# Values of all but the last tile in a loop on TensorE with register addresses, in one column group

## The chip, the cores and the metric

The kernel runs on one core of a Trainium2 chip. The metric is the device time of that core in microseconds (us). Three runs of the kernel before gave 1252.83 us in the median, from 1252.80 to 1253.23 us.

## The reference

Attention with a single query row per head: 8 batches times 32 heads are 256 independent heads, each with one query of 128 numbers and 4096 keys and values, all in bf16.

```python
scale = q.shape[-1] ** -0.5
scores = jnp.einsum('bhqd,bhkd->bhqk', q, k) * scale
attn = _softmax(scores, axis=-1)
return jnp.einsum('bhqk,bhkd->bhqd', attn, v)
```

Keys and values are 268 MB each, and every byte of them is used once. The result has 256 rows of 128 numbers.

## The kernel before

**Tiles.** The work goes in 32 tiles (`NT`) of 8 heads (`G`). In a tile each of the 128 partitions holds 256 keys (`C`) of one head, so that 16 partitions make up a head, and a tile of K or of V is 128 partitions by 32768 bf16 numbers, 8.4 MB. K tiles live in two buffers and V tiles in one (`KB, VB = 2, 1`); only the last V tile is put into a K buffer.

**Scores, in quarters of 64 keys.** For each quarter VectorE multiplies K by the query, in place (L179), and folds the 128 products of a key to 64 (L182), in the first two quarters to 32 (L187). TensorE adds up what is left by matmuls with the identity as weights into a PSUM tile `ps` (`sum_over_d`, L199): four matmuls of 512 columns for each of the first two quarters and eight for each of the last two. VectorE reduces `ps` to scores (`scores_of`, L211). The last three tiles fold to 64 throughout.

**Weights.** When a tile has all its scores, VectorE finds the maximum and the bias (L221 to L232), and ScalarE takes eight exponentials (L240), one per head, into `w`. A partition's weights are zero for the heads that it doesn't belong to.

**Values.** `values_of` (L250 to L268) makes 64 matmuls for a tile. Each takes four keys of every partition: the weights are the 32 columns of `w` for 4 keys times 8 heads, the moving operand is 512 columns of V, and the output is 32 partitions by 512 columns of the PSUM tile `av`. Consecutive matmuls go to four different groups of 32 partitions of `av` (`c0 // CB % TG`), which are four column groups of the array. ScalarE copies `av` to `comb` (L292), and four small matmuls with the selection matrix `pick` (L307) take out the useful quarter-blocks and add the four groups. For every second tile `norm_of` and `recip_of` make the normaliser, and `finish_of` scales the result and stores it now and then.

**Order.** `tc.manual_schedule()` keeps the order of the code on every engine. In the loop over t (L328 to L362) TensorE has, for a tile t: the sums of quarter 0, the query of tile t+1, the sums of quarter 1, the 64 value matmuls of tile t-1, the sums of quarters 2 and 3, and the small matmuls of tile t-1. In tiles 30 and 31 (`v_last`) the values of t-1 come after all four sums. VectorE goes from quarter to quarter, with the reduction of a quarter one quarter behind. SyncE (SP) issues all loads, in the order K(t+1), V(t), K(t+2), V(t+1). V(t) waits until the last value matmul of t-1 has read the single V buffer, K(t+2) until the sums of tile t are through.

Of the kernel before, what the change touches and what calls it, by code (L numbers as in the profile page):

```python
# [7 lines left out]
ACT = mybir.ActivationFunctionType  # L8
# [3 lines left out]
F32 = mybir.dt.float32  # L12

G = 8
KB, VB = 2, 1
TG = 4
R = 2
OB = 4
LAST = 4
NEG = -1.0e30  # L20


@with_exitstack
def kernel(
# [7 lines left out]
    nc = tc.nc  # L32
    B, H, Sq, D = q.shape
    S = k.shape[2]
    P = nc.NUM_PARTITIONS
# [3 lines left out]
    C = S // PH  # L39
    NT = NH // G  # L40
# [5 lines left out]
    CB = 4  # L46
    RG = R * G
    NQ = NT // R
    TB = 32
    AG = CB * G  # L50
    assert TG * AG == P and NH % P == 0 and P % G == 0 and TB % PH == 0 and C % CB == 0

    q_n = q.rearrange("b h o d -> (b h o) d").rearrange("(x p) d -> p x d", p=P)
# [13 lines left out]
    ps_v = ctx.enter_context(tc.tile_pool(name="ps_v", bufs=2, space=bass.MemoryType.PSUM))  # L67
# [9 lines left out]
        out=ident[:], in_=ident[:], pattern=[[-1, P]], compare_op=ALU.not_equal,  # L77
# [32 lines left out]
    for j in range(TG):  # L110
# [17 lines left out]
    nc.gpsimd.memset(w_last[:], 0.0)  # L128

    loads = {}  # L130
    cuts = {
        ("k", 0): [C // 2] * 2,
        ("k", NT - 3): [C // 2] * 2,
# [5 lines left out]
    def load(kind, t):  # L139
        src = k_t if kind == "k" else v_t  # L140
        home = "v" if kind == "v" and t < NT - 1 else "k"
        pool = k_pool if home == "k" else v_pool
        buf = pool.tile([P, C, D], BF16, name=f"{kind}t", tag=home)
        c0 = 0
        for n in cuts.get((kind, t), [C]):
            nc.sync.dma_start(buf[:, c0 : c0 + n, :], src[t, :, c0 : c0 + n, :])  # L146
            c0 += n
            if kind == "k" and t == 0 and c0 == n:
                nc.sync.dma_start(q_all[:], q_n)
        assert c0 == C  # L150
        loads[kind, t] = buf
# [3 lines left out]
    def q_prep(t):  # L155
        x, p0 = divmod(t * G, P)
        qh = ps_q.tile([G, D], F32, name="qh", tag="qp")
        nc.tensor.matmul(  # L158
            qh[:], lhsT=ident[:, p0 : p0 + G], rhs=q_all[:, x, :], start=True, stop=True
        )  # L160
        qg = q_pool.tile([G, D], BF16, name="qg", tag="qg")
        nc.scalar.activation(out=qg[:], in_=qh[:], func=ACT.Copy)  # L162
        qp = ps_q.tile([P, D], F32, name="qp", tag="qp")
        nc.tensor.matmul(qp[:], lhsT=heads[:].rearrange("g h x -> g (h x)"), rhs=qg[:], start=True, stop=True)  # L164
        qb = q_pool.tile([P, 1, D], BF16, name="qb", tag="qb")
        nc.scalar.activation(out=qb[:, 0, :], in_=qp[:], func=ACT.Copy)  # L166
        qbs[t] = qb
# [6 lines left out]
    def product(t, lo, hi):  # L174
        kt = loads["k", t]
        qb = qbs[t]
        for c0 in range(lo, hi, MC):
            part = kt[:, c0 : c0 + MC, :]
            nc.vector.tensor_tensor(  # L179
                out=part, in0=part, in1=qb[:].to_broadcast([P, MC, D]), op=ALU.mult  # L180
            )
            nc.vector.tensor_tensor(  # L182
                out=part[:, :, 0 : D // 2], in0=part[:, :, 0 : D // 2],
                in1=part[:, :, D // 2 : D], op=ALU.add,
            )
            if width_of(t, c0 // UC) < D // 2:
                nc.vector.tensor_tensor(  # L187
                    out=part[:, :, 0 : D // 4], in0=part[:, :, 0 : D // 4],
                    in1=part[:, :, D // 4 : D // 2], op=ALU.add,
                )  # L190
# [3 lines left out]
    def sum_over_d(t, u):  # L194
        kt = loads["k", t]
        ps = ps_s.tile([P, UC, DS], F32, name="ps", tag="ps")
        n = width_of(t, u) // DS
        for s in range(n):
            nc.tensor.matmul(  # L199
                ps[:], lhsT=ident[:],  # L200
                rhs=kt[:, u * UC : (u + 1) * UC, s * DS : (s + 1) * DS],
                start=(s == 0), stop=(s == n - 1),
            )
        sums[t, u] = ps
# [3 lines left out]
    def scores_of(t, u):  # L208
        if u == 0:
            scs[t] = sc_pool.tile([P, C], F32, name="sc", tag="sc")  # L210
        nc.vector.tensor_reduce(  # L211
            out=scs[t][:, u * UC : (u + 1) * UC], in_=sums.pop((t, u))[:], axis=AX.X, op=ALU.add
        )

    ws = {}
# [30 lines left out]
            nc.gpsimd.tensor_copy(out=w_last[:, :, RG - G : RG], in_=w[:, C - LAST : C, :])  # L246

    avs = {}

    def values_of(t, lo, hi):  # L250
        vt = loads["v", t]
        w = ws[t]
        if lo == 0:
            avs[t] = ps_v.tile([P, CB * D], F32, name="av", tag="av")
        end = C if t < NT - 1 else C - LAST


        group = [
            0 if t == NT - 1 and C // 2 <= c0 < C // 2 + 3 * C // 16 else c0 // CB % TG
            for c0 in range(0, end, CB)  # L260
        ]
        for c0 in range(lo, hi, CB):
            i = c0 // CB
            j = group[i]
            nc.tensor.matmul(  # L265
                avs[t][j * AG : (j + 1) * AG, :], lhsT=w[:, c0 : c0 + CB, :],
                rhs=vt[:, c0 : c0 + CB, :], start=(i < TG), stop=(j not in group[i + 1 :]),
            )  # L268
# [6 lines left out]
    def norm_of(n):  # L275
        zp = ps_z.tile([RG, 1], F32, name="zp", tag="zp")
        nc.tensor.matmul(  # L277
            zp[:], lhsT=esums.pop(n).rearrange("p r g -> p (r g)"), rhs=ones[:],
            start=True, stop=True,
        )  # L280
        zps[n] = zp

    def recip_of(n):
        rzs[n] = small.tile([RG, 1], F32, name="rz", tag="rz")
        nc.vector.reciprocal(out=rzs[n][:], in_=zps.pop(n)[:])  # L285
# [3 lines left out]
    def copy_of(t):  # L289
        comb = small.tile([P, CB, D], BF16, name="comb", tag="comb")  # L290
        av = avs.pop(t)[:].rearrange("p (m d) -> p m d", d=D)
        nc.scalar.activation(out=comb[:], in_=av, func=ACT.Copy)  # L292
        combs[t] = comb

    def result_of(t):
        n, r = divmod(t, R)
        comb = combs.pop(t)
        if r == 0:
            ops[n] = ps_o.tile([RG, D], F32, name="op", tag="op")
        if t == NT - 1:  # L300
            for i in range(LAST):
                nc.tensor.matmul(
                    ops[n][:], lhsT=w_last[:, i, :], rhs=loads["v", t][:, C - LAST + i, :],
                    start=False, stop=False,
                )
        for m in range(CB):
            nc.tensor.matmul(  # L307
                ops[n][:], lhsT=pick[:, m, r, :], rhs=comb[:, m, :],
                start=(r == 0 and m == 0), stop=(r == R - 1 and m == CB - 1),
            )  # L310

    def finish_of(n):
        s, u = divmod(n, OB)
        if u == 0:
            stages[s] = o_pool.tile([RG, OB, D], BF16, name="stage", tag="stage")
        nc.scalar.activation(  # L316
            out=stages[s][:, u, :], in_=ops.pop(n)[:], func=ACT.Copy, scale=rzs.pop(n)[:, 0:1]
        )
        last = s == NQ // OB - 1
        if u == OB - 1 or (last and u == OB - 2):  # L320
            lo = u if (last and u == OB - 1) else 0
            nc.scalar.dma_start(o_n[s, :, lo : u + 1, :], stages[s][:, lo : u + 1, :])

    Q = C // 4
    load("k", 0)
    with tc.manual_schedule():
        q_prep(0)
        for t in range(NT):  # L328
            v_last = t >= NT - 2
            n = t // R - 1  # L330
            if t + 1 < NT:
                load("k", t + 1)
            load("v", t)
            product(t, 0, Q)
            sum_over_d(t, 0)
            if t > 2 and t % R == 1:
                recip_of(n)
                finish_of(n)
            if t + 1 < NT:
                q_prep(t + 1)  # L340
            product(t, Q, 2 * Q)
            sum_over_d(t, 1)
            scores_of(t, 0)
            if t > 0 and not v_last:
                values_of(t - 1, 0, C)
                copy_of(t - 1)
            product(t, 2 * Q, 3 * Q)
            sum_over_d(t, 2)
            scores_of(t, 1)
            product(t, 3 * Q, C)  # L350
            sum_over_d(t, 3)
            scores_of(t, 2)
            if t > 0 and v_last:
                values_of(t - 1, 0, C)
            scores_of(t, 3)
            weights_of(t)
            if t > 0:
                if v_last:
                    copy_of(t - 1)
                if t % R == 0:  # L360
                    norm_of(n)
                result_of(t - 1)  # L362
        values_of(NT - 1, 0, C // 2)
        norm_of(NQ - 1)
        recip_of(NQ - 1)
        values_of(NT - 1, C // 2, C - LAST)
        copy_of(NT - 1)
        result_of(NT - 1)
        finish_of(NQ - 1)

# [29 lines left out]
```

## Time and profile before

| | |
|---|---|
| Profiled execution | 1253.24 us; its span (first to last instruction) 1251.5 us |
| TensorE matmul busy | 501.8 us, 40% of the span, 3067 matmuls |
| VectorE busy | 1038.0 us, 83% |
| ScalarE busy | 343.8 us, 27% |
| Moved by DMA | 537.5 MB, mean 429 GB/s |
| Mean granted TensorE clock | 0.638 of full speed |
| Value matmuls, L265 | 2047, together 181.0 us busy |

A group's busy time counts overlapping instructions of an engine once. A matmul's own duration (some 525 ns at L265) is longer than the distance between two of them, since they are pipelined. "Idle before" is the time in which the engine had nothing to do ahead of a group, with what ended it. The engine called SPq is SyncE's queue, from which the loads are issued. The clock is the share of TensorE's full clock that was granted, 0.50 or 1.00 at a given moment.

### The profile page before, as it was taken

To read this page: it belongs to the slowest core of one execution; us is meant where nothing else is said; L and a number is where in the kernel's file an instruction comes from. 1 tells how busy PE (TensorE), PEld (TensorE's weight loads), DVE (VectorE), ACT (ScalarE), POOL (GpSimd) and SP (SyncE) were. 2 spreads that over 40 slices of the span, in tenths; PEclk is the share of its full clock that TensorE was granted. 3 is DMA by queue.
4 is the path that set the end of the run, shared out by engine and by line. 5 is a ranking of instruction groups with operands and counts; after the bars stand their busy time and mean duration, and the time that the engine had idled before them with its cause. 6 is when DMAs were issued, how large, how long until landed. Compare 5 with 4: busy or idle time off the path is not lost.

```text
span 1251.5 us, 7723 instructions
## 1 busy us (share of the span) xinstructions
PE 501.8 (40%) x3067; PEld 176.1 (14%) x3067; DVE 1038.0 (83%) x588; ACT 343.8 (27%) x625; POOL 6.0 (0%) x26
## 2 busy tenths in 40 slices
PE   1334442444333443334533244432444334444455
PEld 0111110111111111111111111111111111111122
DVE  5888898888988889788898888987879888899981
ACT  0321233321333312333123331233321333213333
POOL 1000000000000000000000000000000000000000
PEclk9766655666556666566665666656666566666777
DMA  9999999999999999999999999999999999999997
GB/s 404 436 434 432 436 434 434 434 436 428 426 435 434 436 426 436 429 434 436 434 430 434 432 434 432 428 434 434 436 434 434 434 434 436 434 419 428 428 444 325
DMA packets 11444, 537.50 MB, mean 429 GB/s; under 512 B 1808, under 2 KB 2064, under 8 KB 2320
## 3 DMA queue, kind: packets, MB, share of 16 engines
q1 hardware_dynamic: 11072, 536.94, 99.4%
q8 instruction: 24, 0.39, 0.1%
q10 hardware_dynamic: 336, 0.07, 0.0%
q14 instruction: 12, 0.10, 0.0%
HBM read 536.94 MB, written 0.07 MB: 429 GB/s over the span
## 4 chain that ended last, share of the span: by engine, by line
DMA 76%; PE 15%; DVE 8%; issue 1%; SPq 0%; ACT 0%
DMA vt<-in_v_dram 75%; PE av L265 13%; DVE kt L179 5%; DVE kt L182 2%; PE ps L199 1%; DMA q_all<-in_q_dram 1%; DVE kt L187 0%; DVE sc L211 0%; SPq L146 0%; DVE pmax L221 0%; DVE spread L223 0%; DVE nmax L228 0%; ACT comb L292 0%; PE op L307 0%; ACT stage L316 0%
## 5 line engine op out<-in xcount | busy, mean ns | idle before, releaser
L179 DVE TENSOR_TENSOR kt<-kt,qb 128x8192 bf16<-128x8192 bf16 x128 | 565.1, 4415 | 91.3 <-DMA kt<-in_k_dram 79.8
L199 PE MATMUL ps<-kt,ident 128*128 128x512 bf16 x792 | 293.1, 529 | 662.8 <-DVE kt L187 507.4
L240 ACT ACTIVATE w<-sc,bias 128x256 bf16<-128x256 f32 x256 | 301.1, 1591 | 360.9 <-DVE bias L232 360.9
L182 DVE TENSOR_TENSOR kt<-kt 128x4096 bf16<-128x4096 bf16 x128 | 293.3, 2292 | 4.4
L199 PEld LDWEIGHTS <-ident 128*128 128x128 bf16 x792 | 92.0, 119 | 824.7 <-issue 670.0
L265 PE MATMUL av<-vt,w 128*32 128x512 bf16 x2047 | 181.0, 525 | 43.7 <-DMA vt<-in_v_dram 43.7
L211 DVE TENSOR_REDUCE sc<-ps 128x64 f32<-128x512 f32 x128 | 87.7, 685 | 87.0 <-PE ps L199 87.0
L292 ACT ACTIVATE comb<-av 128x512 bf16<-128x512 f32 x32 | 19.7, 616 | 413.2 <-PE av L265 413.2
L240 ACT ACTIVATION_READ_ACCUMULATOR w<-sc,bias 128x1 f32 x256 | 127.0, 496 | 0.0
L265 PEld LDWEIGHTS <-w 128*32 128x32 bf16 x2047 | 68.1, 127 | 167.7 <-issue 80.9
L187 DVE TENSOR_TENSOR kt<-kt 128x2048 bf16<-128x2048 bf16 x58 | 71.0, 1225 | 2.0
L162 ACT ACTIVATE qg<-qh 8x128 bf16<-8x128 f32 x32 | 8.5, 266 | 95.3 <-PE qh L158 95.3
L307 PE MATMUL op<-comb,pick 128*16 128x128 bf16 x128 | 16.4, 271 | 14.6 <-ACT comb L292 14.6
L221 DVE TENSOR_REDUCE pmax<-sc 128x1 f32<-128x256 f32 x32 | 13.4, 420 | 1.1
L285 DVE RECIPROCAL rz<-zp 16x1 f32<-16x1 f32 x16 | 2.4, 149 | 14.0 <-PE zp L277 14.0
L158 PE MATMUL qh<-q_all,ident 128*8 128x128 bf16 x32 | 8.5, 266 | 13.2 <-DMA q_all<-in_q_dram 13.2
L164 PE MATMUL qp<-qg,heads 8*128 8x128 bf16 x32 | 8.3, 258 | 12.7 <-ACT qg L162 12.7
L307 PEld LDWEIGHTS <-pick 128*16 128x16 bf16 x128 | 9.2, 104 | 26.2 <-issue 26.1
L316 ACT ACTIVATE stage<-op,rz 16x128 bf16<-16x128 f32 x16 | 6.2, 385 | 24.2 <-DVE rz L285 17.8
L166 ACT ACTIVATE qb<-qp 128x128 bf16<-128x128 f32 x32 | 8.9, 277 | 11.1 <-PE qp L164 11.1
L223 DVE TENSOR_SCALAR spread<-same,pmax 128x32 f32<-128x32 f32 x32 | 7.7, 241 | 1.1
L232 DVE TENSOR_SCALAR bias<-own,nmax 128x8 f32<-128x8 f32 x32 | 7.4, 231 | 1.1
(27 smaller groups left out, 26.8 us busy)
## 6 DMA issues: line engine op xcount, KB each, us to landing
kt<-in_k_dram SPq DMA_DIRECT2D x7, 4096.0 KB, 34.4
kt<-in_k_dram SPq DMA_DIRECT2D x2, 2048.0 KB, 36.7
vt<-in_v_dram SPq DMA_DIRECT2D x1, 4096.0 KB, 39.5
vt<-in_v_dram SPq DMA_DIRECT2D x1, 2048.0 KB, 44.0
vt<-in_v_dram SPq DMA_DIRECT2D x1, 1024.0 KB, 46.0
vt<-in_v_dram SPq DMA_DIRECT2D x1, 512.0 KB, 46.8
vt<-in_v_dram SPq DMA_DIRECT2D x31, 33.1
kt<-in_k_dram SPq DMA_DIRECT2D x28, 43.5
```

The lines of the kernel that those rows point to most:

```text
L158: nc.tensor.matmul(qh[:], lhsT=ident[:, p0 : p0 + G], rhs=q_all[:, x, :], start=True, stop=True)
L166: nc.scalar.activation(out=qb[:, 0, :], in_=qp[:], func=ACT.Copy)
L179: nc.vector.tensor_tensor(out=part, in0=part, in1=qb[:].to_broadcast([P, MC, D]), op=ALU.mult)
L182: nc.vector.tensor_tensor(out=part[:, :, 0 : D // 2], in0=part[:, :, 0 : D // 2], in1=part[:, :, D // 2 : D], op=ALU.add,)
L187: nc.vector.tensor_tensor(out=part[:, :, 0 : D // 4], in0=part[:, :, 0 : D // 4], in1=part[:, :, D // 4 : D // 2], op=ALU.add,)
L199: nc.tensor.matmul(ps[:], lhsT=ident[:], rhs=kt[:, u * UC : (u + 1) * UC, s * DS : (s + 1) * DS], start=(s == 0), stop=(s == n - 1),)
L211: nc.vector.tensor_reduce(out=scs[t][:, u * UC : (u + 1) * UC], in_=sums.pop((t, u))[:], axis=AX.X, op=ALU.add)
L221: nc.vector.tensor_reduce(out=pmax[:], in_=sc[:], axis=AX.X, op=ALU.max)
L240: nc.scalar.activation(out=w[:, :, g], in_=sc[:], func=ACT.Exp, bias=bias[:, g : g + 1], scale=scale, accum_out=esum[:, t % R, g : g + 1],)
L265: nc.tensor.matmul(avs[t][j * AG : (j + 1) * AG, :], lhsT=w[:, c0 : c0 + CB, :], rhs=vt[:, c0 : c0 + CB, :], start=(i < TG), stop=(j not i ...
L292: nc.scalar.activation(out=comb[:], in_=av, func=ACT.Copy)
L307: nc.tensor.matmul(ops[n][:], lhsT=pick[:, m, r, :], rhs=comb[:, m, :], start=(r == 0 and m == 0), stop=(r == R - 1 and m == CB - 1),)
```

## The change

The values of tiles 0 to 30 are no longer 64 matmuls written out, but a section made by `values_loop`: two matmuls with fixed addresses, a loop of ten passes with six matmuls each (`LOOP = 6`), and two more with fixed addresses (`EDGE = 2`). In the loop the addresses of the weights and of V come from two registers. All 64 write the same 32 partitions of `av`, so the column groups are no longer changed; the copy to `comb` and the small matmuls with `pick` then take 32 partitions in place of 128. The last tile keeps `values_of`, with the groups as before.

In the built program a pass of the loop has, on TensorE: a register move and a compare-and-branch for the test, seven fused register instructions (six that work out the two addresses of the next matmul, with six register operations each, and one that steps the two registers), the six matmuls with their weights, and a branch back. A section is entered through eight instructions that wait on semaphores: that V has landed, that `w` is there, that all earlier matmuls of TensorE have finished, and that VectorE and ScalarE have come to the instructions that stand before the section in the code (VectorE's last one is the reduction of quarter 0). At its end TensorE waits until its matmuls have finished (a drain) and passes one more wait; the load of the next V waits for the drain. The other engines have one branch each where the section stands, and no wait.

The body of the tile loop is cut anew into `before_values(t)`, `values_loop(t - 1)` and `after_values(t)`, and the written-out order holds for TensorE, VectorE, ScalarE and SP. `behind_loop` adds edges that order products and loads behind the last section for the scheduler alone, without a semaphore. The order on TensorE, VectorE and SP is that of before: the sums of quarters 2 and 3 follow the values of t-1, and K(t+1) and V(t) are issued in this sequence.

```diff
+LOOP = 6
+EDGE = 2
...
+    def values_loop(t):
+
+        vf = loads["v", t][:].rearrange("p c d -> p (c d)")
+        wf = ws[t][:].rearrange("p c g -> p (c g)")
+        avs[t] = ps_v.tile([P, CB * D], F32, name="av", tag="av")
+        av = avs[t][0:AG, :]
+        nv, nw = CB * D, CB * G
+
+        def one(i, **how):
+            pe.matmul(
+                av, lhsT=wf[:, i * nw : (i + 1) * nw], rhs=vf[:, i * nv : (i + 1) * nv], **how
+            )
+
+        with tc.tile_critical() as loop:
+            for i in range(EDGE):
+                one(i, start=(i == 0), stop=False)
+            end = (NV - EDGE) * nw
+            pe.reg_mov(rw, EDGE * nw)
+            pe.reg_mov(rv, EDGE * nv)
+            with pe.While(lambda: pe.snap(rw, min_val=EDGE * nw, max_val=end) < end):
+                ow = pe.snap(rw, min_val=EDGE * nw, max_val=end - LOOP * nw)
+                ov = pe.snap(rv, min_val=EDGE * nv, max_val=(NV - EDGE - LOOP) * nv)
+                for i in range(LOOP):
+                    pe.matmul(
+                        av, lhsT=wf[:, bass.ds(ow + i * nw, nw)],
+                        rhs=vf[:, bass.ds(ov + i * nv, nv)],
+                        start=False, stop=False,
+                    )
+                pe.reg_add(rw, rw, LOOP * nw)
+                pe.reg_add(rv, rv, LOOP * nv)
+            for i in range(NV - EDGE, NV):
+                one(i, start=False, stop=(i == NV - 1))
+        loops.append(loop)
...
-        nc.scalar.activation(out=comb[:], in_=av, func=ACT.Copy)
+        n = P if t == NT - 1 else AG
+        nc.scalar.activation(out=comb[0:n, :, :], in_=av[0:n, :, :], func=ACT.Copy)
...
+        e = P if t == NT - 1 else AG
         for m in range(CB):
             nc.tensor.matmul(
-                ops[n][:], lhsT=pick[:, m, r, :], rhs=comb[:, m, :],
+                ops[n][:], lhsT=pick[0:e, m, r, :], rhs=comb[0:e, m, :],
...
-    with tc.manual_schedule():
-        q_prep(0)
+    with tc.manual_schedule(engines={E.PE, E.DVE, E.Activation, E.SP}):
         for t in range(NT):
...
             if t > 0:
-                if v_last:
-                    copy_of(t - 1)
-                if t % R == 0:
-                    norm_of(n)
-                result_of(t - 1)
+                after_values(t - 1)
+            before_values(t)
+            if t > 0:
+                values_loop(t - 1)
+        after_values(NT - 1)
```

More of the change, by code (lines that the diff above doesn't have):

```diff
@@ L50 @@
     AG = CB * G
+    NV = C // CB
+    assert (NV - 2 * EDGE) % LOOP == 0
     assert TG * AG == P and NH % P == 0 and P % G == 0 and TB % PH == 0 and C % CB == 0
@@ L130, with behind_loop @@
     loads = {}
+    loops = []
+    def behind_loop(made):
+        if loops:
+            tc.add_manual_dep(
+                made.ins, loops[-1].name,
+                mybir.DependencyInfo(
+                    mybir.DependencyClass.NoSync, mybir.DependencyReason.SCHED_ONLY
+                ),
+            )
     cuts = {
@@ L145, in load @@
         for n in cuts.get((kind, t), [C]):
-            nc.sync.dma_start(buf[:, c0 : c0 + n, :], src[t, :, c0 : c0 + n, :])
+            dma = nc.sync.dma_start(buf[:, c0 : c0 + n, :], src[t, :, c0 : c0 + n, :])
+            behind_loop(dma)
             c0 += n
@@ L178, in product @@
             part = kt[:, c0 : c0 + MC, :]
-            nc.vector.tensor_tensor(
+            made = nc.vector.tensor_tensor(
                 out=part, in0=part, in1=qb[:].to_broadcast([P, MC, D]), op=ALU.mult
             )
+            behind_loop(made)
             nc.vector.tensor_tensor(
@@ L248 @@
     avs = {}
+    pe = nc.tensor
+    rv = pe.alloc_register("rv")
+    rw = pe.alloc_register("rw")
+    def values_loop(t):
[22 more added lines that the diff above has]
+                        start=False, stop=False,
+                    )
+                pe.reg_add(rw, rw, LOOP * nw)
[3 more added lines that the diff above has]
+        loops.append(loop)
     def values_of(t, lo, hi):
@@ L324, with before_values, products_end @@
     Q = C // 4
+    def before_values(t):
+        v_last = t >= NT - 2
+        n = t // R - 1
+        if t == 0:
+            q_prep(0)
+        product(t, 0, Q)
+        sum_over_d(t, 0)
+        if t > 2 and t % R == 1:
+            recip_of(n)
+            finish_of(n)
+        if t + 1 < NT:
+            q_prep(t + 1)
+        product(t, Q, 2 * Q)
+        sum_over_d(t, 1)
+        scores_of(t, 0)
+        if v_last:
+            products_end(t)
+    def products_end(t):
+        product(t, 2 * Q, 3 * Q)
+        sum_over_d(t, 2)
+        scores_of(t, 1)
+        product(t, 3 * Q, C)
+        sum_over_d(t, 3)
+        scores_of(t, 2)
@@ L325, with after_values @@
+    def after_values(t):
+        v_last = t >= NT - 2
+        if t > 0 and not v_last:
+            copy_of(t - 1)
+        if t + 1 < NT:
+            load("k", t + 1)
+        load("v", t)
+        if not v_last:
+            products_end(t)
+        scores_of(t, 3)
+        weights_of(t)
+        if t > 0:
+            if v_last:
+                copy_of(t - 1)
+            if t % R == 0:
+                norm_of(t // R - 1)
+            result_of(t - 1)
     load("k", 0)
-    with tc.manual_schedule():
-        q_prep(0)
+    E = mybir.EngineType
@@ L328 @@
+    with tc.manual_schedule(engines={E.PE, E.DVE, E.Activation, E.SP}):
         for t in range(NT):
[L329 to L345, printed above, removed]
-                copy_of(t - 1)
[L347 to L356, printed above, removed]
-            if t > 0:
-                if v_last:
-                    copy_of(t - 1)
-                if t % R == 0:
-                    norm_of(n)
-                result_of(t - 1)
+            if t > 0:
+                after_values(t - 1)
@@ L363 @@
+            before_values(t)
+            if t > 0:
+                values_loop(t - 1)
+        after_values(NT - 1)
         values_of(NT - 1, 0, C // 2)
```

## The prediction

> **What bounds the kernel now.** I read the slices of the span first. Outside the first and last slice the transfers stand at 9 tenths throughout, TensorE at 2 to 4, VectorE at 8.
>
> ```profile
> PE   1334442444333443334533244432444334444455
> DVE  5888898888988889788898888987879888899981
> PEclk9766655666556666566665666656666566666777
> DMA  9999999999999999999999999999999999999997
> ```
>
> So the kernel runs at the speed of its loads: 537 MB at about 434 GB/s. Next the chain of work that ended last, from the middle of the kernel: each V load follows the value matmuls that free the only V buffer, and the next values follow that load.
>
> ```profile
> 606.94 6.02 PE av L265 x34
> 612.97 0.02 issue
> 612.99 32.62 DMA vt<-in_v_dram
> 645.60 0.04 issue
> 645.65 5.45 PE av L265 x63
> ```
>
> The period is 645.65 - 606.94 = 38.7 us, and 16.8 MB at 434 GB/s is 38.7 us too. The load takes 32.6 us and not 19.3 because a K load is still ahead of it: that K lands by 626.3 (the product of the next tile starts at 626.34, below), 13.3 us after V was issued. Values could end so much later before the transfers ran dry. That is the first slack, and it isn't the one that decides. The second lies between TensorE and VectorE. The timeline of one tile:
>
> ```profile
> 626.34 4.43 DVE L179 TENSOR_TENSOR kt<-kt,qb 128x8192 bf16<-128x8192 bf16 x1 [2.96 <-DMA kt<-in_k_dram]
> ...
> 634.27 4.42 DVE L179 TENSOR_TENSOR kt<-kt,qb 128x8192 bf16<-128x8192 bf16 x1
> ...
> 642.19 0.68 DVE L211 TENSOR_REDUCE sc<-ps 128x64 f32<-128x512 f32 x1
> 642.33 1.87 PE L199 MATMUL ps<-kt,ident 128*128 128x512 bf16 x4 [5.18 <-DVE kt L187]
> ```
>
> VectorE waits 2.96 us for K before a tile, then needs 7.93 and 7.92 us for a quarter. Today the values (6 us) end before VectorE has made the products of quarters 2 and 3 (13.4 us), so the sums queued behind the values aren't late.
>
> Last, the distance between value matmuls, by stretch. Columns: stretch, length, TensorE busy (count, those that straddle an edge included), ScalarE, granted clock, DMA share, GB/s.
>
> ```profile
> 606.90:608.60 1.70, 1.66 (x16) 0.00 (x0) 0.50 1.34 554
> 608.60:610.30 1.70, 1.70 (x20) 0.00 (x0) 0.50 0.80 347
> 610.30:612.00 1.70, 1.70 (x24) 0.00 (x0) 0.57 1.07 463
> 612.00:612.90 0.90, 0.90 (x20) 0.00 (x0) 1.00 1.18 510
> ```
>
> Sixteen matmuls start in 1.70 us at clock 0.50, four at a time: 0.427 us a step. At clock 1.00 a step is about 0.22 us. The clock goes up some 4.5 us after the burst begins. The end of the kernel before even has one column group: of the 28 matmuls from 1243.30 on, twelve go to group 0 and sixteen to four groups, 16 steps, at clock 1.00.
>
> ```profile
> 1243.30 3.61 PE L265 MATMUL av<-vt,w 128*32 128x512 bf16 x28
> 1156.01 3.63 PE L199 MATMUL ps<-kt,ident 128*128 128x512 bf16 x16
> ```
>
> 3.61/16 = 0.226 us for a step, the last drain included: one group costs a full step per matmul. The second row gives 16 sums at full clock, 3.63 us.
>
> [...]
>
> **The change part by part.**
>
> *One column group.* 64 matmuls are now 64 steps, not 16. The mean burst of values lasts 5.84 us (181.0/31), so (5.84 - 16 x 0.216)/0.211 = 11 of its steps are cold; I take 10[...]. 10 x 0.427 + 54 x 0.216 = 15.9 us if the array sets the pace.
>
> *Register addresses.* A pass has seven fused register instructions, six weight loads, six matmuls, a move, a compare-and-branch and a branch.[...] Ten passes 17.2, the four outer matmuls 1.3, last drain 0.4: **L = 19 us**.[...]
>
> *Entry and exit.* VectorE's reduction of quarter 0 (0.68 us) is awaited in addition; it hides beside the four sums of quarter 1 (1.87 us) and would cost at most 0.7 without them. Eight wait instructions, drain and NoOp: nothing below zero, above perhaps 2 us; I take 0.3 and 0.5.
>
> *What queues behind.* On TensorE the 16 sums of quarters 2 and 3, for which VectorE's last reductions, the next tile's products, the next sums and so the next loop wait. On SP the V load, with K behind it. From the end of one loop to the start of the next: exit 0.5; 16 sums 3.63; last reduction to next product 1.94 (reduction at 660.08, bias done at 662.02); two quarters 15.85; four sums and a handshake 2.0; entry 0.3. Sum 24.2 us. The period becomes the larger of 38.7 and L + 24.2, so the change is hidden only up to L = 14.5. The V path[...] is L + 21.6 and doesn't bind; the K load, queued after the sums, lands about 41 us after a loop ends and is wanted 6 us after the next one ends, so it is in time.
>
> *Shorter copy and small matmuls.* The copy's 128 partitions become 32 with the same 512 columns each[...]. Both nothing, and off the path. *Fewer instructions to fetch*: the instruction queues moved 0.49 of 537.5 MB, at most 1.1 us, and only while loads bind.[...]
>
> *Sum.* The first values start at about 66.5 us (first V load freed at 72.19, less 6). The loop of tile 28 ends at 66.5 + 29 L + 28 x 24.2 = 744 + 29 L; before, 1156. Then 5.9 us to tile 30's products, its four quarters at 6.7 us with reductions and last sums 32.5 us, the loop of tile 29 L, two V loads 40.7 us, and the end after the last landing 4.4 us as today: 83.5 + L. Span = 828 + 30 L. With L = 19: 1398, plus the 1.74 us that the profiled execution has around its span: **1400 us**. The profiled execution (1253.24) is 0.4 us above the median shown (1252.83), which I neglect.
>
> **The rivals.**
>
> *The array sets the pace* (register work is hidden by the matmuls): L = 16.3, 828 + 489 + 2 = 1319 us. For it: all queued weight loads hide behind matmuls today.[...]
>
> *Costly register work*: L between 23.5 and 32, 1535 to 1790 us. It includes the case that TensorE, being paced, isn't granted its full clock: 64 x 0.427 + 0.7 = 28 us, 1670.[...]
>
> *No slower.* If the sums of quarter 1 just ahead have already brought the full clock, and register work is hidden, L = 64 x 0.216 + 0.4 = 14.2, under the 14.5 from which it decides. The loads then bind as before; V(30) is issued 9 us later but K(31) covers 10 of them. Left is the last loop, ending at 1242.8 in place of 1232.5, of which the warm clock gives back most: about 1.4 us, 1254.6 us. Against it: those four sums run at 0.43 us a step, cold, and the shortest burst behind four sums, 5.03 us, still had 7 cold steps (same formula).
>
> [...]
>
> **How the numbers follow.** Sequencer-paced with L of 17 to 23 (1340 to 1520): 46%. Array-paced (1290 to 1340, 25 us allowed for the formula): 27%. Costly register work (1520 to 1800): 20%. No slower: 4%. A fetch per pass: 3%. The range 1285 to 1690 leaves out the no-slower case, the fetch and the upper third of the costly one, about 14%. Measurement tells this kernel from no change at about 0.2%, 2.5 us. Faster than that needs all 1.1 us of the fetch and more: 1%. Same: 3%. Slower: 96%.
>
> **What would show it.** In the profile after: the transfers at some 8 tenths; the period of V loads at 43 us; VectorE waiting some 6 us per tile for the sums of quarter 2 or 3, and hardly ever for K; the loop's matmuls spaced 0.28 us, with clock 1.00 in most of the loop and a longer gap after every sixth. Spacing of 0.216 proves the array-paced rival, 0.427 at clock 0.50 the clock. I am wrong if VectorE can finish a tile without the sums behind the loop, or if the period is not L + 24.

## The result

The kernel after takes 1357.2 us in the median of four runs (1356.33 to 1360.91), the kernel before 1252.95 us (1252.80 to 1253.23). The ratio is 1.0837, 95% interval 1.0817 to 1.0858: 104 us, 8.4%, slower. The profiled execution took 1360.91 us, its span is 1359.2 us, 107.7 us longer than the span before.

Slices of the span after, as shown of before:

```profile
PE   1366755566745567545665555666555675557646
DVE  5877798777796777887777877778977679876760
PEclk9688766788757887767886767877767877777768
DMA  9989999999998999998988999999999899999683
```

TensorE is busy more than half as much again as before (787.5 us, 501.8 before), VectorE for the same time in a longer span, and the transfers now have slices under 9 tenths: 395 GB/s over the span where it was 429. The chain of work that the profile can follow back from the end covers only the last 10 us here, so the waits and the timeline have to carry the reading. Two waits of VectorE before (who waited for whom, us in total, times, longest):

```profile
DVE sc L211 <- PE ps L199: 87.0, 34, 3.1
DVE kt L179 <- DMA kt<-in_k_dram: 79.8, 25, 4.3
```

And four waits after:

```profile
DVE sc L229 <- PE ps L217: 248.9, 61, 12.1
PE av L280 <- DMA out_dram<-stage: 18.2, 3, 6.2
PE av L280 <- POOL w_last L264: 12.0, 1, 12.0
DVE kt L196 <- ACT qb L183: 11.5, 1, 11.5
```

VectorE's reductions waited 87.0 us for the sums before and wait 248.9 us now. Its 79.8 us of waiting for K are gone; the last row is the one wait for the first query. The two rows between are waits at the entry of a section that the prediction didn't have. The copy and the small matmuls took what they took before, as forecast: a copy 0.59 us for 32 partitions and 0.60 for 128, four small matmuls 0.39 us (L364 at 624.07, and L307 at 1159.57 before).

One loop in the timeline (start, length, engine, line, what; PEld is the weight loads of TensorE, PEq its sequencer), and the start of the next:

```profile
603.31 1.03 PE L280 MATMUL av<-vt,w 128*32 128x512 bf16 x2 [2.11 <-PEq L284]
...
604.13 15.40 PE L294 MATMUL av<-vt,w 128*32 x60
...
613.51 0.97 PEld L294 LDWEIGHTS av<-vt,w 128*32 x6 [0.53 <-issue]
615.05 0.97 PEld L294 LDWEIGHTS av<-vt,w 128*32 x6 [0.56 <-issue]
616.56 0.97 PEld L294 LDWEIGHTS av<-vt,w 128*32 x6 [0.54 <-issue]
618.07 0.97 PEld L294 LDWEIGHTS av<-vt,w 128*32 x6 [0.53 <-issue]
...
620.36 0.33 SPq L162 DMA_DIRECT2D vt<-in_v_dram  x1
620.39 3.61 PE L217 MATMUL ps<-kt,ident 128*128 128x512 bf16 x16 [0.20 <-PEq L284]
...
622.31 0.69 DVE L229 TENSOR_REDUCE sc<-ps 128x64 f32<-128x512 f32 x1 [8.52 <-PE ps L217]
...
625.88 4.42 DVE L196 TENSOR_TENSOR kt<-kt,qb 128x8192 bf16<-128x8192 bf16 x1
...
644.22 1.04 PE L280 MATMUL av<-vt,w 128*32 128x512 bf16 x2 [0.44 <-PE ps L217]
...
647.99 8.52 PEld L294 LDWEIGHTS av<-vt,w 128*32 x40 [0.23 <-issue]
```

From the first value matmul to the V load that the section frees are 17.05 us; in the next tile it is 16.43 (644.22 to 660.65). In the loop at 644.22 the weight loads from 645.05 to 647.61 come 0.427 us apart, at a granted clock of 0.50, and the 40 after them 0.216 us apart (8.52 us), at 1.00. I read the 40 as a backlog of TensorE's instructions that had built up at the lower clock; the trace doesn't show that queue itself. After them passes of the loop start 1.51 to 1.54 us apart: six weight loads close together, then a gap of 0.53 to 0.56. VectorE stands 8.52 us before the sums of quarter 2 come. From 620.36 to the next section's first matmul at 644.22 are 23.86 us.

A chain of waits that comes back to its own start once a tile is called a ring below; no period can be shorter than a ring. The ring of the sums is loop, 16 sums, VectorE, sums of the next tile, loop: 16.4 + 23.9 = 40.3 us. A second one, the ring of V, is loop, load of the next V into the single buffer, loop. Which of the two ends last shows at the start of a section: issue times plus times to landing give 1.11 us as the shortest time from V's landing to the first matmul in the runs with sections and V in one tile, and 0.43 us from the (modelled) end of the last sum. Of the sections of tiles 1 to 28, 16 begin 0.43 to 0.47 us after the last sum, so the sums released them (the one at 644.22 is one: V had landed at 643.0); 9 begin 1.11 to 1.15 us after V has landed, later after the sums (the one at 603.31, V landed at 602.2); three wait for a store. Both rings are at work here.

Where the 107.7 us of the two spans are, by the issue times of the V loads:

| | before | after | more |
|---|---|---|---|
| to the load freed by the first values | 72.19 | 85.01 | 12.8 |
| 28 periods from there | 1083.9 (38.7 each) | 1154.4 | 70.5 |
| from the load after tile 28's values to the end | 95.4 | 119.8 | 24.4 |

Of the 70.5 us, 28 x (40.3 - 38.7) = 45 are the plain period, 17 are three periods of 45.8 to 46.2 us (the store), and 9 are spread over the rest, most of it in a few periods of 41 to 42.5 us. In the longest, of 41.6 to 42.5, V released the section; the V loads of these three took 24.1 to 24.4 us to land, where the median is 22.5. Why a load takes longer in some tiles wasn't found.

### The profile page after: what moved, and what is told of

The parts are those of the page before. It is cut to its first block, busy times and chain, and to the rows that moved or that the text cites. A ratio compares the mean times of both kernels' runs of the same rounds, so it can differ in the third digit from the quotient of the medians.

```text
span 1359.2 us, 11319 instructions
## 1 busy us (share of the span) xinstructions
PE 787.5 (58%) x3067; PEld 298.0 (22%) x3067; DVE 1038.2 (76%) x588; ACT 341.4 (25%) x625; POOL 6.0 (0%) x26
## 5 line engine op out<-in xcount | busy, mean ns | idle before, releaser
L217 PE MATMUL ps<-kt,ident 128*128 128x512 bf16 x792 | 252.3, 474 | 483.9 <-DVE kt L205 427.8
L294 PE MATMUL av<-vt,w 128*32 x1860 | 459.2, 403 | 3.6
L229 DVE TENSOR_REDUCE sc<-ps 128x64 f32<-128x512 f32 x128 | 88.0, 688 | 248.9 <-PE ps L217 248.9
L294 PEld LDWEIGHTS av<-vt,w 128*32 x1860 | 188.1, 101 | 280.9 <-issue 123.4
L217 PEld LDWEIGHTS <-ident 128*128 128x128 bf16 x792 | 85.2, 110 | 620.4 <-issue 567.5
L348 ACT ACTIVATE comb<-av 32x512 bf16<-32x512 f32 (+1 forms) x32 | 18.8, 587 | 743.9 <-PEq L284 737.8
L280 PE MATMUL av<-vt,w 128*32 128x512 bf16 x124 | 50.4, 498 | 53.6 <-DMA out_dram<-stage 18.2
L280 PEld LDWEIGHTS av<-vt,w 128*32 128x32 bf16 x124 | 7.8, 101 | 95.6 <-issue 94.6
L179 ACT ACTIVATE qg<-qh 8x128 bf16<-8x128 f32 x32 | 8.5, 267 | 38.9 <-PE qh L175 38.9
L181 PE MATMUL qp<-qg,heads 8*128 8x128 bf16 x32 | 8.3, 258 | 12.8 <-ACT qg L179 12.8
L364 PE MATMUL op<-comb,pick 32*16 32x128 bf16 (+1 forms) x128 | 12.3, 215 | 1.7 <-ACT comb L348 1.7
L364 PEld LDWEIGHTS <-pick 32*16 32x16 bf16 (+1 forms) x128 | 6.7, 83 | 9.0 <-issue 8.6
## 6 DMA issues: line engine op xcount, KB each, us to landing
vt<-in_v_dram SPq DMA_DIRECT2D x1, 1024.0 KB, 38.9
vt<-in_v_dram SPq DMA_DIRECT2D x31, 22.5
```

The costliest lines, as they stand in the source:

```text
L217: nc.tensor.matmul(ps[:], lhsT=ident[:], rhs=kt[:, u * UC : (u + 1) * UC, s * DS : (s + 1) * DS], start=(s == 0), stop=(s == n - 1),)
L229: nc.vector.tensor_reduce(out=scs[t][:, u * UC : (u + 1) * UC], in_=sums.pop((t, u))[:], axis=AX.X, op=ALU.add)
L280: pe.matmul(av, lhsT=wf[:, i * nw : (i + 1) * nw], rhs=vf[:, i * nv : (i + 1) * nv], **how)
L294: pe.matmul(av, lhsT=wf[:, bass.ds(ow + i * nw, nw)], rhs=vf[:, bass.ds(ov + i * nv, nv)], start=False, stop=False,)
L348: nc.scalar.activation(out=comb[0:n, :, :], in_=av[0:n, :, :], func=ACT.Copy)
L364: nc.tensor.matmul(ops[n][:], lhsT=pick[0:e, m, r, :], rhs=comb[0:e, m, :], start=(r == 0 and m == 0), stop=(r == R - 1 and m == CB - 1),)
```

## The experiments

Every run stands beside runs of the kernel before (1252.9 to 1253.0 us in the median). "Period" is the mean over 28 tiles, from the issue of V loads.

**Taking the change apart.** The first run has the kernel before with all 64 value matmuls of tiles 0 to 30 in one column group, fixed addresses, no section (the copy and the small matmuls take 32 partitions, as in the kernel after):

```diff
-            0 if t == NT - 1 and C // 2 <= c0 < C // 2 + 3 * C // 16 else c0 // CB % TG
+            0 if t < NT - 1 or C // 2 <= c0 < C // 2 + 3 * C // 16 else c0 // CB % TG
...
-                rhs=vt[:, c0 : c0 + CB, :], start=(i < TG), stop=(j not in group[i + 1 :]),
+                rhs=vt[:, c0 : c0 + CB, :], start=(i < (TG if t == NT - 1 else 1)), stop=(j not in group[i + 1 :]),
```

> The kernel before with one edit: the 64 value matmuls of tiles 0 to 30 all go to one column group, written out with fixed addresses, no section, no registers. Theory (a ring of values, the 16 sums behind them, VectorE, the next sums): the values take about 16 us, the rest of the ring 23.4 us, a period of 39.3 us in place of 38.7, and a longer first and last burst: 1275 to 1295 us. Rival (the register addresses and the section are what costs, one column group is hidden): 1252 to 1258 us.

1284.2 us, ratio 1.0246 (1.0229 to 1.0263), period 39.3. One column group alone costs 31 us; it isn't hidden. The wait of VectorE for the sums is there without any loop:

```profile
DVE sc L211 <- PE ps L199: 194.5, 61, 6.9
PE av L265 <- DMA vt<-in_v_dram: 18.0, 24, 1.9
```

The second row says more: 24 of the bursts waited for V. The chain of work from the middle of this run goes through V alone:

```profile
594.22 23.93 DMA vt<-in_v_dram
618.15 0.04 issue
618.20 16.57 PE av L265 x64
634.77 0.02 issue
634.78 24.24 DMA vt<-in_v_dram
```

So the time fell in the expected range, but not by the ring that the theory named: 24 of the 28 bursts begin 0.04 to 0.05 us after V has landed, only four right behind the sums. With the medians of a burst and of a load, 15.5 + 23.8 = 39.3 us, the ring of V is the period. That the 39.3 us worked out for the ring of the sums are the same number is luck.

The second run has the section of the kernel after with the loop written out, one column group:

```diff
         with tc.tile_critical() as loop:
-            for i in range(EDGE):
-                one(i, start=(i == 0), stop=False)
...
+            for i in range(NV):
+                one(i, start=(i == 0), stop=(i == NV - 1))
```

> The kernel after with the loop written out inside the section: 64 matmuls with fixed addresses, still one column group. Theory (the two limits of the burst, array and sequencer, nearly coincide): little is gained, 1335 to 1352 us, bursts of about 16 us. Rival (register work costs): 1300 us or less.

1341.8 us, 1.0703 (1.0685 to 1.0721), period 40.8. So of the change's 104 us, 31 come from the column group, 58 from putting such a burst into a section, and 15 from the loop with its registers, in this order of the steps. The 58 are 60 between the two spans: 18 in three periods of 45.6 to 46.6 us (the stores), 18 in the end, 12 of them the wait for the weights of tile 31, 1 at the start, and the remaining 24 are some 0.85 us in every period. For these the trace offers the entry: a burst begins 0.04 us after V has landed in the run before and never sooner than 1.11 us after it here. Which of the waiting instructions takes that time was not tested.

The third run is the same section with the four column groups of before:

```diff
-        av = avs[t][0:AG, :]
+        av = [avs[t][j * AG : (j + 1) * AG, :] for j in range(TG)]
...
+            for i in range(NV):
+                one(i, start=(i < TG), stop=(i >= NV - TG))
```

(with `av[i % TG]` as the output, and the copy and the small matmuls on 128 partitions).

> The kernel after with the loop written out inside the section and the four column groups of before. Theory: bursts of 6 us, the ring is short again, the section's waits are hidden while the loads bind, and only the end is later because the last section waits for the weights of tile 31: 1254 to 1262 us. Rival (entry and exit of the section cost by themselves): over 1280 us.

1258.6 us, 1.0043 (1.0028 to 1.0057), period 38.7. A section that costs 58 us around bursts of 16 us costs 6 us around bursts of 5.7. It has the same waits at its entry:

```profile
PE av L280 <- PEq L284: 64.0, 24, 6.5
PE av L280 <- DMA out_dram<-stage: 14.0, 3, 5.1
PE av L280 <- POOL w_last L264: 12.0, 1, 12.0
```

TensorE waits for the stores and for the weights of tile 31 here too, but in the periods the slack that the prediction counted (13.3 us for the next V) takes the wait up, the 1.1 us behind V's landing included; of the 6 us of the two spans, 4 are in the end of the kernel and 2 before the first freed V. The price of a wait was set by the slack that the long burst had used up.

**The loop's two limits.** Twenty passes of three matmuls, and two of thirty (`LOOP = 3`, `LOOP = 30` in place of 6):

> The kernel after with 20 passes of three matmuls in place of ten of six. Theory (the sequencer paces the loop: about 0.16 us per matmul and 0.55 us per pass): a pass of 1.03 us, the loop 5 us longer, 30 loops: 1490 to 1530 us. Rival (the array paces it): no change, 1357 us.

> The kernel after with two passes of thirty matmuls. Theory: the sequencer needs some 11 us and the array then paces the loop with about 16 us, where it has 16.4 now: 1335 to 1352 us. Rival (each register-addressed matmul costs more than a step of the array): no change, 1357 us.

1529.1 us, 1.2202 (1.2181 to 1.2222), and 1340.5 us, 1.0711 (1.0679 to 1.0742). In the run with passes of three, they start 1.00 to 1.05 us apart, 1.03 in the mean of the seven from 640.48 us:

```profile
641.53 0.82 PE L294 MATMUL av<-vt,w 128*32 x3 [0.23 <-issue]
...
642.53 0.82 PE L294 MATMUL av<-vt,w 128*32 x3 [0.19 <-issue]
...
643.58 0.82 PE L294 MATMUL av<-vt,w 128*32 x3 [0.23 <-issue]
```

A pass of six takes 1.51 us, so by my estimate from the two runs a matmul with its address work is (1.51 - 1.03)/3 = 0.16 us and what a pass has besides is 1.03 - 3 x 0.16 = 0.55 us. Passes of seven, in a run further down, start 1.66 to 1.70 us apart, where this gives 1.67. A single matmul with register addresses therefore fits under a step of the array (the 0.216 us of the 40 weight loads above, at full clock), but six of them with what a pass has besides (1.51 us) don't fit under six steps (1.30 us). With passes of thirty the same estimate gives 2 x (30 x 0.16 + 0.55) = 10.7 us, and the run is as fast, within the spread of its executions (1337.2 to 1345.6), as the one with fixed addresses in the same section (1341.8): register addresses as such cost nothing that shows here, ten passes cost 15 to 17 us.

**The waits of the section.** The store of the results, issued by ScalarE before a section, moved behind it; in another run the weights of a tile ordered behind the section, as `behind_loop` does it for products and loads:

```diff
+    def store_of(n):
...
+            dma = nc.scalar.dma_start(o_n[s, :, lo : u + 1, :], stages[s][:, lo : u + 1, :])
+            behind_loop(dma)
...
         if t > 0 and not v_last:
             copy_of(t - 1)
+        if t > 2 and t % R == 1:
+            store_of(t // R - 1)
```

> The kernel after with the store of the results issued behind the section that follows it, not before. Theory (three sections each wait some 6 us for a store to land): 18 us less, 1336 to 1342 us. Rival (the wait for the store only takes the place of another wait): 1350 us or more.

```diff
-        nc.vector.tensor_reduce(out=pmax[:], in_=sc[:], axis=AX.X, op=ALU.max)
+        made = nc.vector.tensor_reduce(out=pmax[:], in_=sc[:], axis=AX.X, op=ALU.max)
+        behind_loop(made)
```

> The kernel after with the weights of a tile ordered behind the preceding section for the scheduler, so that the last section no longer waits for the weights of tile 31. Theory: the last section starts at the end of the sums, some 11 us earlier: 1343 to 1349 us. Rival (the end is set by the loads): 1355 us or more.

1329.4 us, 1.0616 (1.0596 to 1.0635): 28 us less than the kernel after, not 18, and below the expected range. The three long periods are gone, all 28 lie between 40.2 and 41.4, and the last section no longer waits for the weights of tile 31 either:

```profile
1298.71 0.69 DVE L229 TENSOR_REDUCE sc<-ps 128x64 f32<-128x512 f32 x1 [3.06 <-PE ps L217]
...
1301.18 1.03 PE L280 MATMUL av<-vt,w 128*32 128x512 bf16 x2 [2.51 <-issue]
...
1310.25 0.21 POOL L264 COPY w_last<-w 128x32 bf16<-128x32 bf16 x1 [1303.15 <-ACT w L258]
```

With the store moved, the weights of tile 31 stand behind the last section too (`w_last` is copied at 1310, after it began at 1301). The weights alone: 1345.2 us, 1.0730 (1.0712 to 1.0748), 12 us less. So both waits are real, and the first edit had taken away both. That shows in the run with both:

> The kernel after with the store and the weights both ordered behind the section. Theory (the two waits lie in different tiles and add up): 1357 - 28 - 12 = 1317 us, 1311 to 1323; a period of 40.3 us, from the ring of loop, sums and VectorE. Rival (another wait takes their place): 1330 us or more.

1330.1 us, 1.0612 (1.0594 to 1.0629), period 40.5, the same as with the store alone and outside the expected range. My sum of 28 and 12 counted the end twice. What is left, 77 us over before, is the period of 40.5 us (51 us) and a start and an end that are 13 us longer each.

**Which ring sets the period.** If it is the ring of the sums alone, then an earlier place for the loop, after the sums of quarter 0, should give VectorE more to do meanwhile:

```diff
         product(t, 0, Q)
         sum_over_d(t, 0)
...
-        product(t, Q, 2 * Q)
-        sum_over_d(t, 1)
-        scores_of(t, 0)
         if v_last:
             products_end(t)

     def products_end(t):
+        product(t, Q, 2 * Q)
+        sum_over_d(t, 1)
+        scores_of(t, 0)
         product(t, 2 * Q, 3 * Q)
         sum_over_d(t, 2)
-        scores_of(t, 1)
         product(t, 3 * Q, C)
         sum_over_d(t, 3)
+        scores_of(t, 1)
         scores_of(t, 2)
```

> The kernel after, the loop unchanged but placed earlier: after the sums of quarter 0 and not of quarter 1, so that VectorE has three quarters of products to make while the loop runs; the reduction of quarter 1 moves behind the product of quarter 3. Theory: the ring is the loop plus some 17 us, under 38.7, so the loads bind again except at the end: 1260 to 1285 us although the loop is as long as before. Rival (the length of the loop itself, through the single V buffer, sets the period): about 1357 us.

1364.6 us, 1.0866 (1.0812 to 1.0919), period 41.6. My theory failed here: nothing was gained. In its timeline TensorE is free at 634.4 us, and the section still starts only at 642.89:

```profile
617.23 0.33 SPq L162 DMA_DIRECT2D vt<-in_v_dram  x1
...
642.89 1.03 PE L280 MATMUL av<-vt,w 128*32 128x512 bf16 x2 [8.48 <-PEq L284]
```

25.7 us after the V load was issued. It was waiting for V: 25 of this run's sections begin 1.11 to 1.27 us after V has landed and 5.6 us or more after the sums; the other three wait for a store. The transfers had run dry before that load: stretches of this run (length, busy time of TensorE, its weight loads, VectorE, ScalarE, GpSimd, then clock, DMA share, GB/s):

```profile
610.00:616.00 6.00, 6.00 (x30) 2.60 (x27) 3.11 (x2) 0.00 (x0) 0.00 (x0) 1.00 1.19 513
616.00:618.00 2.00, 1.63 (x8) 0.53 (x7) 0.00 (x0) 0.59 (x1) 0.00 (x0) 1.00 0.12 41
618.00:643.00 25.00, 6.62 (x31) 2.57 (x29) 22.34 (x16) 10.09 (x19) 0.00 (x0) 0.65 0.99 417
```

The ring of V stands right behind the ring of the sums. A load of V takes 22.5 us to landing in the kernel after and 23.4 in this run (medians), and the first matmul follows 1.1 us later: the ring is some 16.4 + 22.5 + 1.1 = 40.0 us in the kernel after, against 40.3 for the sums, and 16.4 + 23.4 + 1.1 = 40.9 us here, where the periods without a store average 41.0. Opening one ring alone can't help. That theory was tested by opening each ring and both, without the section's waits for store and weights. For the V ring, V in two half tiles with a section of 32 matmuls each, so that half of the next V may be loaded when half of the values are through:

```diff
-LOOP = 6
+LOOP = 7
...
+            for h in range(2):
+                half = v_pool.tile([P, C // 2, D], BF16, name="vt", tag=f"v{h}")
+                dma = nc.sync.dma_start(half[:], src[t, :, h * C // 2 : (h + 1) * C // 2, :])
...
+        for h in range(2):
+            vf = loads["v", t][h][:].rearrange("p c d -> p (c d)")
...
+            with tc.tile_critical() as loop:
```

> As f1, with V in two half tiles and a section of 32 matmuls for each (four passes of seven), so that the first half of the next V can be loaded when half of the values are through. Theory of two rings of nearly the same length: the ring of the sums still binds and gets longer by a second entry and exit, some 1 to 1.5 us a tile: 1335 to 1365 us. Rival (the single V buffer alone sets the period): 1290 us or less.

> As f1, with the loop after the sums of quarter 0 as in the run of that name. Theory of two rings: the ring of the sums is short now, that of the V buffer (loop 16.5 us, load 23.5 us to landing) binds with about 40 us: 1305 to 1330 us. Rival (only the ring of the sums matters, and the last run was held up by the store alone): 1285 us or less.

> As f3, with V in halves as in f2: both rings are opened. Theory of two rings: the loads bind again with 38.7 us a tile, though TensorE works on values some 17 us a tile as in the kernel after: 1256 to 1280 us. Rival (something else in the section or the loop sets the period): 1300 us or more.

| | loop after quarter 1 | loop after quarter 0 |
|---|---|---|
| V in one tile | 1330.1, period 40.5 | 1334.1 (ratio 1.0591 to 1.0660), period 41.1 |
| V in halves | 1354.9 (1.0793 to 1.0829), period 41.4 | 1281.1 (1.0209 to 1.0243), period 38.9 |

Neither alone gains, both together gain 49 us. The two single openings also part the rings. With V in halves alone every tile's first section begins 0.43 to 0.57 us after the last sum, when its half of V has long landed: only the ring of the sums is left, longer by the second section's entry (1.3 us at least between the two bursts). With the early place alone all 28 sections begin 1.11 to 1.27 us after V's landing, and 5.7 us or more after the sums: only the ring of V is left, and 16.4 + 23.4 + 1.1 = 40.9 us is within 0.2 us of its period. Its 1334.1 us lie 4 us above the expected range.

In the last run the period is within 0.2 us of before, though a tile's values still take two loops of one column group. It is the loads that bind again (stretch, length, the engines as above, clock, DMA share, GB/s; before, 433 GB/s in the same part of the kernel, in the other three runs of the table 405 to 414):

```profile
112.60:1161.70 1049.10, 655.89 (x2570) 248.31 (x2570) 881.56 (x499) 286.57 (x527) 0.00 (x0) 0.80 1.00 432
```

TensorE waits for them:

```profile
PE av L292 <- DMA vt<-in_v_dram: 43.6, 16, 4.8
```

Each first section begins 0.35 to 1.0 us after the second half of V has landed, and 2.0 us or more after the last sum, which suggests that the section waits for both halves (not tested): the halves free the buffer earlier but don't let the values begin earlier. Of its 28 us over before, 6 are in the periods, some 9 in the start and 12 in the end, by the issue of the second half of V, which is the one that waits for the last value matmul. It came out 1 us above the top of its expected range. No version tried is faster than the kernel before. A loop over four column groups was not tried, so its worth stays open.

## Why the prediction was right

*The bound and the mechanism.* Right as far as it goes. The load-bound kernel has slack for a short burst of values only, and the 16 sums queued behind the burst make a ring with VectorE. The part outside the loop was put at 24.2 us and measured 23.86; reductions waiting for the sums and no wait for K were forecast and seen. But this ring releases only 16 of the 28 sections; in 9 it is the ring of V, which the prediction set aside.

*L, the length of the loop.* The mis-sized term. I had L = 19 with ten passes of 1.72 us; measured, 1.51 to 1.54 and 16.4 to 17.05. The 1.72 us, and the length of the loop in the rival of costly register work, were my estimate: no trace before the change has a matmul with register addresses or a loop. The runs put a matmul with its weight load and address work at some 0.16 us and what a pass has besides at some 0.55; what a single instruction of these takes they don't show. The size of L is that of the array-paced rival (16.3), but not for its reason: while the clock is at 0.50 a pass of six at the later 1.51 us, 0.25 us a matmul, would be ahead of the array's 0.427 us a step, and at full clock the matmuls come 0.216 apart until the last passes run at 1.51 us (the backlog, as I read it). The loop ends with passes that the array doesn't pace (1.51 us, where six of its steps are 1.30). So the periods of the kernel after are 40.2 to 40.3 us again and again, and with fixed addresses in the same section, where a burst takes 14.6 to 16.9 us, 38.6 to 42.4 outside the stores' periods.

*Entry and exit.* I took 0.8 us, a guess that no trace had behind it, and hid the waits of the entry. What failed is the list of what is awaited, which is that of the description of the change: V, `w`, the earlier matmuls, and the instructions of VectorE and ScalarE. The runs show that the entry waits for a store put in order before it and, at the last section, for the weights of tile 31. 17 us for three stores and 12 us for these weights were missing. The entry was put at 0.3 us; behind the sums it is 0.43, behind V 1.1.

*The sum.* 828 + 30 L with the measured 16.4 gives 1320 us for the span; it was 1359. Some 39 us of waits and a longer end were missing, and L was 2.6 us too long, 78 us over 30 loops. The two errors oppose each other, and that 1400 came within 3.2% of 1357 is partly luck. So is the case it fell in: 1357 us lie where the sequencer-paced loop was put, but that case had L at 17 to 23, and L is 16.4. In the end of the kernel I had the loads set the pace; in the trace TensorE does, with 10.4 us of work after the last loop where 4.4 were counted.

*The V path.* "L + 21.6 and doesn't bind" was the weakest step. Of its 21.6 us, 19.3 are the bytes at the rate of the loads; the other 2.3 were my estimate, without a trace behind it. A V load took 22.5 us to landing, and the 1.1 us from landing to the first matmul were left out: L + 23.6, against L + 23.9 for the ring of the sums. For the time it made little difference, at most the 9 us of the longer periods; for what to mend it made all: the run that opened only the ring I believed in gained nothing.

*The rivals.* "No slower" needed L under 14.5; the shortest loop took 16.2. Costly register work and a fetch per pass, which no run had shown, are excluded by the passes' 1.51 us, and the case without the full clock by the granted clock, 1.00 over the last 8 us of each of the 31 loops.

## What to carry to other kernels

Ask of a longer burst on an engine that is idle more than half the time what is queued behind it, and follow every ring it lies in: here two, 0.3 us apart, and only opening both brought most of the time back. To tell which ring binds, look at what ended last before each burst, not at the mean period: the run with one column group had the period forecast for one ring and was held by the other. The waits at the entry cost little while there was slack to take them up: the same section cost 6 us around short bursts and 58 around long ones. In a loop count passes, not instructions: with ten passes the fixed part was 15 to 17 us of the kernel's time, with two it was hidden.

## What the runs showed of the hardware

- Passes of the loop started 1.00 to 1.05 us apart with three matmuls with register addresses (mean 1.03), 1.51 to 1.54 with six, 1.66 to 1.70 with seven: by estimate from these some 0.16 us for a matmul with its weight load and address work, and 0.55 us for what belongs to a pass (test, step, branch).
- In the loop starting at 644.22 us weight loads came 0.427 us apart at a granted clock of 0.50, then 40 of them 0.216 us apart at 1.00, and only the last passes started 1.51 us apart.
- A store of 16 KB took 13.7 us to land among loads of 8.4 MB (median of three in the kernel after), long enough to hold up a section that waits for it by 5.9 to 6.2 us.
- A V load of 8.4 MB issued at the end of a long burst lands 22.1 to 23.9 us after its issue (medians of the kernel after and of nine other runs with V in one tile), 2.8 to 4.6 us more than its bytes at 434 GB/s.
- With V in one tile, the first matmul of a section came 1.11 us after V's landing at the soonest and 0.43 us after the last sum; without a section (the kernel before, and one column group written out) 0.04 us after the landing.
